# Block-sparse attention with an ELU feed-forward network: all 24 key blocks under a mask, or only the eight that a query block sees

## The chip, the cores and the metric

One core of a Trainium2 chip runs the whole program. The metric is device time in microseconds; lower is better. PE is TensorE, DVE VectorE, ACT ScalarE, POOL GpSimd, SP SyncE, which here only issues DMAs.

## What is computed

```python
B, H, S, D = 4, 8, 768, 64            # block = 32, so 24 blocks
scores = q @ k.T / sqrt(D)
mask = |blk_i - blk_j| <= 1           # neighbours
mask |= blk_i in (0, 23) or blk_j in (0, 23)
mask |= blk_j in sampled_blocks[blk_i]     # three drawn blocks per query block
attn = softmax(where(mask, scores, -1e9))
x = (attn @ v) as [3072 tokens, 512]
out = ELU(x @ w_in) @ w_out           # 512 -> 2048 -> 512
```
A query block from 1 to 22 sees at most eight key blocks: three neighbours, the first and the last, and three drawn ones, which may repeat others. Blocks 0 and 23 see all 24. The weights come as float64, the rest as float32; `sampled_blocks` is data, known only when the program runs.

## The kernel before

Every float32 operand of a product is held as two float16 parts, a high and a low one, and three of the four part products are summed. A batch has six tiles of 128 queries; two tiles are a chunk, so there are twelve chunks of 256 tokens. Work is queued by step with a rank within the step (`Steps`), and from step 40 on the order of emission is the order of issue on each engine. A chunk is 16 steps, one tile of one head each:

- `scores`: 128 queries against all 768 keys in four products, two key ranges by two parts of q. The two parts of k lie on the 128 rows with q twice.
- `sm_min` on DVE adds the mask and takes the row's minimum (scores come negated); `sm_exp` on ACT makes exp and its sum; `sm_hi` on ACT and `sm_lo` on DVE make the two parts of p, scaled by the reciprocal of the sum.
- `to_pT` transposes both parts of p with one DMA on SP's queue. `av_part` multiplies by v for a pair of heads: a first part with full array, a second with the two heads in the two column halves of the array (lines 365 and 371). `av_part3` is an earlier form for the first 32 tiles (line 348).
- `ffn_h`, `ffn_act1` to `ffn_act5` and `ffn_o` are the FFN of a chunk that is some ten steps behind: per chunk 192 products of 256 columns (line 426) and 96 of 512 (line 465).
- `load_w`, `w_bits1`, `w_bits2`, `w_split` turn a piece of the float64 weights into two float16 parts, 32 pieces, one per step in the first steps. `prep_k1/2`, `prep_v1/2`, `prep_q1/2` split the operands; k and q are transposed by DMA.
- `build_mask` and `expand_mask` make a mask of 128 queries by 768 keys for each tile of a batch, once.

Of the kernel before, what the change touches and what calls it, by code (L numbers as in the profile page):

```python
# [7 lines left out]
F32 = mybir.dt.float32  # L8
F16 = mybir.dt.float16
BF16 = mybir.dt.bfloat16  # L10
I32 = mybir.dt.int32
# [4 lines left out]
WINDOW = 1  # L16
# [3 lines left out]
class Steps:  # L20
    """Work queued by step; within a step the lower rank is issued first."""
# [16 lines left out]
    def left(self):  # L38
        return bool(self.work)


@with_exitstack
def kernel(
# [19 lines left out]
    NT = S // P            # query tiles (and key chunks) of a batch  # L63
    CT = 2                 # query tiles of a chunk
    NCH = NT // CT         # chunks of a batch
    NPAIR = H // 2
    DM, DFF = w_in.shape
# [3 lines left out]
    NB = S // BLOCK  # L71
    NR = sampled.shape[1]
    CW = CT * P            # tokens of a chunk
    HS = S * 2 // 3

    QS, KS, VS = -2.0, 16.0, 32.0
    SS = 2.0 ** 8          # scores come out as -SS * s
# [6 lines left out]
    assert abs(QS * KS) == SS / 8.0 and D == 64  # L84

    const = ctx.enter_context(tc.tile_pool(name="const", bufs=1))
    kvp = ctx.enter_context(tc.tile_pool(name="kvp", bufs=4))
    work = ctx.enter_context(tc.tile_pool(name="work", bufs=2))
    ps_s = ctx.enter_context(tc.tile_pool(name="ps_s", bufs=2, space=bass.MemoryType.PSUM))
    ps_a = ctx.enter_context(tc.tile_pool(name="ps_a", bufs=1, space=bass.MemoryType.PSUM))  # L90
    ps_f = ctx.enter_context(tc.tile_pool(name="ps_f", bufs=3, space=bass.MemoryType.PSUM))

    gs_col = const.tile([P, 1], F32, tag="gs", name="gs")
    nc.gpsimd.memset(gs_col, GS)
    st = Steps()
    chunks = [(b, c) for b in range(B) for c in range(NCH)]
    GSTEPS = 2 * CT        # steps of a (chunk, pair) group
    groups = [(t, hp) for t in range(len(chunks)) for hp in range(NPAIR)]
    NSTEP = len(groups) * GSTEPS

# [1 line left out]
    eqmb = work.tile([P, 2, S], BF16, tag="pT", bufs=4, name="eqmb")  # L102
    eq, mb = eqmb[:, 0, :], eqmb[:, 1, :]
    mask = const.tile([P, NT, S], BF16, tag="mask", name="mask")

    def build_mask():
        samp = const.tile([P, NR, 2], I32, tag="samp", name="samp")
# [3 lines left out]
        blk = const.tile([P, 3, NB], F32, tag="blk", name="blk")  # L111
        bi, bf, al = blk.bitcast(I32)[:, 0, :], blk[:, 1, :], blk[:, 2, :]
        nc.gpsimd.iota(bi, pattern=[[1, NB]], base=0, channel_multiplier=0)
        nc.gpsimd.memset(al, 1.0)
        for sg in (1, -1):
            nc.gpsimd.affine_select(
                al, al, pattern=[[sg, NB]], compare_op=ALU.is_ge, fill=0.0,
                base=WINDOW, channel_multiplier=-sg)
        for e in (0, NB - 1):
            nc.gpsimd.memset(al[:, e : e + 1], 1.0)  # L120
            nc.gpsimd.affine_select(
                al, al, pattern=[[0, NB]], compare_op=ALU.not_equal, fill=1.0,
                base=-e, channel_multiplier=1)
        # eq: 1 where the token (column) lies in the block (partition)
        nc.gpsimd.memset(eq, 1.0)
        eq3 = eq.rearrange("p (c k) -> p c k", c=NT)
        for sg, base in ((1, 0), (-1, BLOCK - 1)):
            nc.gpsimd.affine_select(
                eq3, eq3, pattern=[[sg, NT], [sg * NT, P]], compare_op=ALU.is_ge, fill=0.0,
                base=base, channel_multiplier=-sg * BLOCK)  # L130
        na = const.tile([P, P], BF16, tag="na", name="na")
        nc.gpsimd.memset(na, 0.0)
        nc.vector.tensor_copy(bf, bi)
        sf = const.tile([P, NR], F32, tag="sf", name="sf")
        nc.vector.tensor_copy(sf, samp[:, :, 0])
        for r in range(NR):
            nc.vector.scalar_tensor_tensor(
                al, bf, sf[:, r : r + 1], al, op0=ALU.is_equal, op1=ALU.add)
        nc.vector.tensor_scalar(na[:, :NB], al, 0.0, None, op0=ALU.is_le)
        # mb: rows key blocks, columns query tokens  # L140
        pm = ps_s.tile([P, 1024], F32, tag="s", name="pm")
        for n0, n1 in ((0, HS), (HS, S)):
            nc.tensor.matmul(pm[:, n0:n1], lhsT=na, rhs=eq[:, n0:n1], start=True, stop=True)
        nc.scalar.activation(mb, pm[:, :S], AF.Copy)

    def expand_mask(c):
        pm = ps_s.tile([P, 1024], F32, tag="s", name=f"pm{c}")
        for n0, n1 in ((0, HS), (HS, S)):
            nc.tensor.matmul(
                pm[:, n0:n1], lhsT=mb[:, c * P : (c + 1) * P], rhs=eq[:, n0:n1],  # L150
                start=True, stop=True)
        nc.scalar.activation(mask[:, c, :], pm[:, :S], AF.Copy, scale=NEG * SS)

# [1 line left out]
    wih, wil, woh, wol, wst = {}, {}, {}, {}, {}  # L155

    def load_w(i):
        f = i % NFC
        s = work.tile([P, 512, 2], I32, tag="wst", bufs=2, name=f"wst{i}")
# [9 lines left out]
    wu, wx = {}, {}  # L169

    def w_bits1(i):
        # 2^-111 on the upper word, read as float32, takes 888 off its exponent
        # field of 11 bits: what is left is the float32 field of 2^8 w.
        wu[i] = work.tile([P, 512], F32, tag="e", bufs=3, name=f"wu{i}")
        nc.scalar.activation(wu[i], wst[i].bitcast(F32)[:, :, 1], AF.Copy, scale=2.0 ** -111)
# [21 lines left out]
    kst, vst, qst = {}, {}, {}  # L197
    kT, vS, qT = {}, {}, {}

    def load_kv(b, hp, src, dst, nm):  # L200
        s = work.tile([P, 2 * NT, D], F32, tag="kvst", bufs=2, name=f"{nm}st{b}_{hp}")
        nc.sync.dma_start(
            s.rearrange("p (j c) d -> p j c d", j=2),
            src[b, 2 * hp : 2 * hp + 2].rearrange("j (p c) d -> p j c d", c=NT))
        dst[b, hp] = s

    nat = {}
# [7 lines left out]
    def prep_k1(b, hp):  # L215
        n = work.tile([P, 2 * NT, 2, D], F16, tag="knat", bufs=1, name=f"kn{b}_{hp}")
        nat["k", b, hp] = n
        hi_part(n[:, :, 0, :], kst[b, hp], KS)

    def prep_k2(b, hp):  # L220
        n = nat.pop(("k", b, hp))
        lo_part(n[:, :, 1, :], kst.pop((b, hp)), n[:, :, 0, :], KS)
        t = kvp.tile([P, 2 * NT, P], F16, tag="kT", name=f"kT{b}_{hp}")
        nc.sync.dma_start_transpose(t, n.rearrange("p a h d -> p (a h d)"))
        kT[b, hp] = t
# [3 lines left out]
    def v_part(t, j, hl):  # L229
        return t[:, j * NT : (j + 1) * NT, hl ^ j, :]  # L230

    def prep_v1(b, hp):
        t = kvp.tile([P, 2 * NT, 2, D], F16, tag="vS", name=f"vS{b}_{hp}")
        for j in range(2):
            hi_part(v_part(t, j, 0), vst[b, hp][:, j * NT : (j + 1) * NT, :], VS)
        vS[b, hp] = t

    def prep_v2(b, hp):
        t, s = vS[b, hp], vst.pop((b, hp))
        for j in range(2):  # L240
            lo_part(v_part(t, j, 1), s[:, j * NT : (j + 1) * NT, :], v_part(t, j, 0), VS)

    def load_q(t, hp):
        b, c = chunks[t]
        s = work.tile([P, 2 * CT, D], F32, tag="qst", name=f"qst{t}_{hp}")
        nc.sync.dma_start(
            s.rearrange("p (j c) d -> p j c d", j=2),
            q[b, 2 * hp : 2 * hp + 2].rearrange("j (p c) d -> p j c d", c=NT)[
# [367 lines left out]
```

## Time and profile before

| | |
|---|---|
| median of 3 runs | 874.04 us (873.43 to 877.04) |
| span of the profiled execution | 874.6 us |
| PE busy | 771.8 us (88%) |
| DVE busy | 728.7 us (83%) |
| ACT busy | 614.0 us (70%) |
| POOL busy | 213.1 us (24%) |
| DMA, SP's queue | 130.06 MB, 76.3% of 16 engines |
| mean granted clock of PE | 0.951 |

How to read it: the busy shares of the engines hold stages with different limits; the slices of the page and the windows show which engine is full when. PE's busy time comes from modelled ends of products that overlap, so the pace is read from the starts or from a run of many. An idle engine's wait is put down to what ended last.

### The profile page before, as it was taken

The page shows a single profiled execution, that of the slowest core. Times are in us where ns is not written, and L with a number is a line of the kernel's source. Part 1 is how long each engine was busy: PE and PEld are TensorE (multiplying, and loading weights), DVE is VectorE, ACT ScalarE, POOL GpSimd, SP SyncE. Part 2 cuts the span into 40 slices and gives each one's busy share as a digit, 9 for nine tenths or more (in the row PEclk, how much of TensorE's full clock was granted, in tenths as well). Part 3 has the DMA queues.
Part 4 walks back from the last instruction along what each step waited for, and adds up shares of the span by engine and source line. Part 5 has one row for each costly group of instructions (what it writes and reads, how often), then busy time and mean ns, then how long its engine had stood idle before and what let it go on. Part 6 is the DMA issues. An engine that isn't in the chain of part 4 may idle for free.

```text
span 874.6 us, 15351 instructions
## 1 busy us (share of the span) xinstructions
PE 771.8 (88%) x5486; PEld 505.9 (58%) x5486; DVE 728.7 (83%) x1526; ACT 614.0 (70%) x1088; POOL 213.1 (24%) x170
## 2 busy tenths in 40 slices
PE   2455457889987999999979999999989999999998
PEld 0123245447745756757746757758548658567583
DVE  5999999998997887987997988969989969879130
ACT  5866567778877867867767867767878769677140
POOL 3565656620210210210210211301201202103030
PEclk9765688999999999999999999999999999999999
DMA  8998989779999587799997778699897786776000
GB/s 223 244 213 196 200 186 218 182 161 157 183 215 207 101 146 151 119 165 181 178 191 158 139 145 140 121 186 170 164 226 145 134 160 124 144 140 108 23 13 25
DMA packets 412912, 137.33 MB, mean 157 GB/s; under 512 B 379044, under 2 KB 407716, under 8 KB 412836
## 3 DMA queue, kind: packets, MB, share of 16 engines
q1 hardware_dynamic: 409380, 130.06, 76.3%
q10 hardware_dynamic: 3456, 6.29, 2.3%
q8 instruction: 43, 0.70, 0.3%
q14 instruction: 33, 0.27, 0.1%
HBM read 35.65 MB, written 6.29 MB: 48 GB/s over the span
## 4 chain that ended last, share of the span: by engine, by line
PE 50%; DVE 14%; DMA 4%; ACT 2%; issue 1%; ACTq 0%; DVEq 0%
PE o L465 19%; PE h L426 18%; PE s L281 7%; DVE p L319 5%; PE av L365 4%; DMA pT<-p 4%; DVE t L290 3%; PE av L371 2%; DVE e L444 1%; DVE gh L449 1%; DVE kn L213 1%; DVE xf L405 1%; DVE vS L213 1%; ACT t L297 1%; ACT p L307 0%
## 5 line engine op out<-in xcount | busy, mean ns | idle before, releaser
L454 POOL TENSOR_TENSOR gl<-e,gh 128x512 f16<-128x512 f32 x96 | 121.2, 1263 | 572.6 <-DVE gh L449 446.6
L307 ACT ACTIVATE p<-t,sum 128x768 f16<-128x768 f32 x168 | 157.0, 934 | 122.9 <-DVE sum L303 90.2
L290 DVE CUSTOM_DVE_ANT_0 t<-s,mask 128x768 f32<-128x768 f32 x192 | 182.5, 951 | 52.7 <-PE s L281 51.5
L281 PE MATMUL s<-kT,qT 128*128 128x512 f16 (+1 forms) x768 | 167.2, 343 | 58.3 <-DVE m L290 39.2
L426 PE MATMUL h<-xl,wih 128*128 128x256 f16 x768 | 210.7, 275 | 2.6 <-DVE xl L389 2.6
L426 PE MATMUL h<-xh,wih 128*128 128x256 f16 x768 | 209.6, 274 | 3.6 <-DVE e L444 2.0
L426 PE MATMUL h<-xh,wil 128*128 128x256 f16 x768 | 210.8, 275 | 0.0
L319 DVE SCALAR_TENSOR_TENSOR p<-t,sum,p 128x768 f16<-128x768 f32 x168 | 208.2, 1239 | 1.5 <-ACT p L307 1.5
L297 ACT ACTIVATE t<-t,m 128x768 f32<-128x768 f32 x192 | 177.2, 923 | 7.9 <-DVE m L290 7.7
L426 PEld LDWEIGHTS <-wih 128*128 128x128 f16 x1536 | 149.5, 98 | 27.8 <-issue 9.7
L281 PEld LDWEIGHTS <-qT 128*128 128x128 f16 x768 | 76.5, 101 | 125.5 <-issue 41.5
L465 PE MATMUL o<-wol,gh 128*128 128x512 f16 x384 | 145.8, 380 | 1.0 <-POOL wol L194 1.0
L465 PE MATMUL o<-woh,gh 128*128 128x512 f16 x384 | 146.0, 380 | 0.1
L465 PE MATMUL o<-woh,gl 128*128 128x512 f16 x384 | 145.8, 380 | 0.0
L465 PEld LDWEIGHTS <-gh 128*128 128x128 f16 x768 | 73.6, 98 | 77.0 <-issue 4.5
L444 DVE SCALAR_TENSOR_TENSOR e<-h,e 128x512 f32<-128x512 f32 x96 | 66.0, 688 | 34.3 <-ACT e L440 33.6
L426 PEld LDWEIGHTS <-wil 128*128 128x128 f16 x768 | 75.7, 99 | 12.3 <-issue 3.0
L365 PE MATMUL av<-pT,vS 128*128 128x256 f16 x480 | 62.9, 279 | 13.2 <-DMA pT<-p 13.1
L440 ACT ACTIVATE e<-e,gs 128x512 f32<-128x512 f32 x96 | 69.3, 722 | 2.9
L434 ACT ACTIVATE e<-h 128x512 f32<-128x512 f32 x96 | 55.9, 582 | 19.0 <-PE h L426 14.5
L465 PEld LDWEIGHTS <-gl 128*128 128x128 f16 x384 | 37.6, 98 | 45.9 <-issue 1.3
L365 PEld LDWEIGHTS <-vS 128*128 128x128 f16 x480 | 47.3, 100 | 22.4 <-DMA pT<-p 14.1
(59 smaller groups left out, 782.2 us busy)
## 6 DMA issues: line engine op xcount, KB each, us to landing
wst<-in_moe_w_in_dram SPq DMA_DIRECT2D x16, 512.0 KB, 4.5
wst<-in_moe_w_out_dram SPq DMA_DIRECT2D x16, 512.0 KB, 4.1
qst<-in_q_dram SPq DMA_DIRECT2D x48, 128.0 KB, 3.0
kst<-in_k_dram SPq DMA_DIRECT2D x16, 384.0 KB, 3.8
vst<-in_v_dram SPq DMA_DIRECT2D x16, 384.0 KB, 3.9
out_dram<-r ACTq DMA_DIRECT2D x24, 256.0 KB, 3.2
pT<-p SPq DMA_TRANSPOSE x192, 4.0
qT<-qn SPq DMA_TRANSPOSE x48, 3.4
```

Source lines behind the costliest of these rows:

```text
L281: nc.tensor.matmul(ps[:, n0:n1], lhsT=qT[t, hp][:, (j * CT + c) * 2 + hl, :], rhs=kk[:, n0:n1], start=(hl == 0), stop=(hl == 1))
L290: nc.vector.tensor_tensor_reduce(ts_, pS.pop(i)[:, :S], mask[:, chunks[t][1] * CT + c, :], op0=ALU.add, op1=ALU.min, scale=1.0 / SS, scala ...
L297: nc.scalar.activation(tS[i], tS[i], AF.Exp, bias=mS.pop(i), scale=-1.0, accum_out=s)
L307: nc.scalar.activation(p[:, 0, :], tS[i], AF.Copy, scale=sumS[i])
L319: nc.vector.scalar_tensor_tensor(p[:, 1, :], tS.pop(i), sumS.pop(i), p[:, 0, :], op0=ALU.mult, op1=ALU.subtract)
L365: nc.tensor.matmul(o[:, j, :], lhsT=vv[:, j * NT + kc, :, :].rearrange("p h d -> p (h d)"), rhs=pT[t, hp, j][:, kc, :], start=(kc == 0 and ...
L426: nc.tensor.matmul(ps[:, e, :], lhsT=w[2 * f + e][:, cs], rhs=x[t][:, cc, :], start=(n == 0), stop=(n == 3 * NCC - 1))
L434: nc.scalar.activation(e, hS[t, f], AF.Exp, scale=IH)
L440: nc.scalar.activation(e, e, AF.Relu, bias=gs_col, scale=-GS)
L444: nc.vector.scalar_tensor_tensor(e, hS.pop((t, f)), -IH * GS, e, op0=ALU.mult, op1=ALU.min)
L454: nc.gpsimd.tensor_tensor(g, eS.pop((t, f)), gh[f], op=ALU.subtract)
L465: nc.tensor.matmul(o, lhsT=g[f][:, e, ms], rhs=w[2 * f + e], start=(f == 0 and e == 0 and n == 0), stop=(f == NFP - 1 and e == 1 and n == 2))
```

## The change

Attention is written anew; the FFN, the weights' conversion and the splitting into two parts stay as they are in their arithmetic.

- Tokens 32 to 735 of a batch (blocks 1 to 22) are cut into six units of four query blocks, the last with two; the first and last block go apart (`special`), as 64 queries against all keys. A unit (`unit`) handles four heads: two pairs, each with one head on rows 0 to 63 and one on rows 64 to 127.
- `gather_k` copies, for each query block and drawn block, 32 keys of the transposed k next to each other on DVE. The place comes from a register, loaded from the list of drawn blocks (`block_of`). `gather_v` does the same for v with a DMA from a scratch tensor in device memory into `vg`; v is split first and stored there (`store_v`).
- `scores` has one product for each query block, head and part, on 64 rows by 32 columns of the array, against 96 neighbour keys, 64 edge keys or 96 drawn keys. `attn_v` has one for each query block, head and half of the 256 keys, on 128 rows by 32 columns.
- A row of p has 256 keys instead of 768. Its division by the sum moves behind the product with v (`norm`). The mask shrinks to eight values per query.
- The order of issue is fixed from the start. A chunk is still 256 tokens and 16 steps; its FFN begins 21 steps after its attention.

```diff
+    def block_of(eng, qb, r):
+        c = qb * NR + r
+        return eng.value_load(idx[0:1, c : c + 1], min_val=0, max_val=NB - 1)
...
+    def gather_v(b, u, i):
+        qb = 1 + QB * u + i
+        t = vg[slot[b, u]]
+        nc.sync.dma_start(t[0:96, 0, i], scr[b][(qb - 1) * BLOCK : (qb + 2) * BLOCK, :])
+        for r in range(NR):
+            n = block_of(nc.sync, qb, r)
+            nc.sync.dma_start(
+                t[32 + 32 * r : 64 + 32 * r, 1, i], scr[b][bass.ds(n * BLOCK, BLOCK), :])
+
+    def gather_k(b, u, qd):
+        n = blocks_in(u)
+        t = work.tile([P, 4, QB * NR * BLOCK], F16, tag="kR", name=f"kR{b}_{u}_{qd}")
+        kR[b, u, qd] = t
+        for c in range(n * NR):
+            x = block_of(nc.vector, 1 + QB * u + c // NR, c % NR)
+            nc.vector.tensor_copy(
+                t[:, :, c * BLOCK : (c + 1) * BLOCK],
+                kT[b, qd][:, :, bass.ds(x * BLOCK, BLOCK)])
...
+    def scores(b, u, qd):
...
+        for pp in range(2):
+            for part in range(3):
+                for ql, kl in PROD:
+                    kb = kk[:, 2 * pp + kl, :]
+                    for i in range(n):
+                        w0 = (QB * u + i) * BLOCK
+                        for j in range(2):
+                            js = slice(64 * j, 64 * j + 64)
...
+                            nc.tensor.matmul(
+                                ps[32 * i : 32 * i + 32, j, pp, c0:c1],
+                                lhsT=qT[b, u][
+                                    js, 2 * (2 * qd + pp) + ql, q0 + 32 * i : q0 + 32 * i + 32],
+                                rhs=m, start=(ql + kl == 0), stop=(ql == 1))
...
+    def attn_v(b, u, qd):
...
+                for e in range(6):
+                    ab, (pl, vl) = e // 3, PROD[e % 3]
+                    for i in range(n):
+                        nc.tensor.matmul(
+                            o[32 * i : 32 * i + 32, h, :],
+                            lhsT=t[:, pl * 8 + (2 * j + pp) * 2 + ab, 32 * i : 32 * i + 32],
+                            rhs=vv[:, ab, i, h, vl, :], start=(e == 0), stop=(e == 5))
...
+    LEAD = 21
+    NSTEP = 2 * NFP
+    E0 = 8
...
+        st.at(s - 1, 3.0, lambda: gather_k(b, u, qd))
+        st.at(s, 0, lambda: scores(b, u, qd))
+        st.at(s, 5, lambda: sm_min(b, u, qd))
+        st.at(s, 6, lambda: sm_exp(b, u, qd))
+        st.at(s + 1, 3.1, lambda: sm_hi(b, u, qd))
+        st.at(s + 1, 3.2, lambda: sm_lo(b, u, qd))
+        st.at(s + 1, 8, lambda: sm_T(b, u, qd))
+        st.at(s + 4, 1, lambda: attn_v(b, u, qd))
```

On DVE, one tile in the steady part before: minimum and its value, the reciprocal of the sum, the low part of p.

```order
L290 ISA t_4521,m_4522<-s_4468,mask 128x768
L290 ISA m_4522 128x1
L302 TENSOR_SCALAR sum_4512<-sum_4512 128x1
L303 RECIPROCAL sum_4512<-sum_4512 128x1
L319 SCALAR_TENSOR_TENSOR p_4510<-t_4440,sum_4462,p_4510 128x768
```
On DVE now, around the gather for a half unit in the second batch (`kR` is the gathered k; the load, the two checks, the address step and the copy stand six times for a half unit, twelve for a full one):

```order
L364 ISA t_4_1_9839,m_4_1_9840<-s_4_1_9661,mask 128x256
L364 ISA m_4_1_9840 128x1
L564 SCALAR_TENSOR_TENSOR e_3_9905<-h_3_9806,e_3_9905 128x512
L569 CAST gh_3_9909<-e_3_9905 128x512
L120 TENSOR_LOAD idx
L120 ISA x2
L318 ISA
L318 COPY kR_5_0_9913<-kT_0_5853 128x4x32
L394 SCALAR_TENSOR_TENSOR p_4_1_9974<-t_4_1_9839,p_4_1_9974 128x1024
```
The minima shrink from 768 to 256 columns, and the register loads and copies come between the FFN's work and the low part of p.

On SP's queue before, in the steady part, transpositions of p, k and q with an operand's load between:

```order
L314 DMA_TRANSPOSE pT_4601<-p_4603 128x12x128
L224 DMA_TRANSPOSE kT_0_4669<-kn_0_4607 128x12x128
L202 DMA kst_1_4677<-in_k_dram 128x2x384
L314 DMA_TRANSPOSE pT_4736<-p_4671 128x12x128
L263 DMA_TRANSPOSE qT_0_4740<-qn_0_4675 128x8x128
```
And now, where the gathers of v for a unit (`vg`) stand among the transpositions:

```order
L402 DMA_TRANSPOSE pT_5_0_10292<-p_5_0_10289 128x16x64
L306 DMA vg_80<-scr_4704 96x1024
L120 TENSOR_LOAD idx
L120 ISA x2
L309 ISA
L309 DMA vg_80<-scr_4704 32x1024
L280 DMA_TRANSPOSE qT_2_10571<-qn_2_10500 128x8x128
```
The load, the checks, the address step and the gather stand three times for each query block; the transpositions queue behind them.

On PE before, one tile's scores between the FFN's products (rows that only repeat are left out; there are four pairs of load and product):

```order
L465 LDWEIGHTS gl_1_4766
L465 MATMUL o_1_5205<-woh_997,gl_1_4766 128x512
L281 LDWEIGHTS qT_1_4992
L281 MATMUL s_5226<-kT_1_4921,qT_1_4992 128x512
L281 MATMUL s_5226<-kT_1_4921,qT_1_4992 128x256
L465 LDWEIGHTS gh_2_4820
```
And now a full unit's scores, followed by the product with v of an earlier unit (144 and 96 pairs):

```order
L546 MATMUL h_6_12286<-xT_9625,wil_1277 128x256
L351 LDWEIGHTS qT_3_11681
L351 MATMUL s_3_1_12447<-kT_1_5855,qT_3_11681 32x96
L351 MATMUL s_3_1_12447<-kT_1_5855,qT_3_11681 32x64
L351 MATMUL s_3_1_12447<-kR_3_1_12319,qT_3_11681 32x96
L417 LDWEIGHTS pT_3_0_12236
L417 MATMUL av_3_12592<-vg_81,pT_3_0_12236 32x64
```
Where four wide pairs stood at each step, a block of 288 short rows and one of 192 stand at one step of four. PE has 29582 rows in all, before 10974.

More of the change, by code (lines that the diff above doesn't have):

```diff
@@ L15 @@
 BLOCK = 32
-WINDOW = 1
 NEG = 1e9
@@ L91 @@
     ps_f = ctx.enter_context(tc.tile_pool(name="ps_f", bufs=3, space=bass.MemoryType.PSUM))
+    ctx.enter_context(tc.manual_schedule())
+    st = Steps()
     gs_col = const.tile([P, 1], F32, tag="gs", name="gs")
     nc.gpsimd.memset(gs_col, GS)
[L95 to L102, printed above, removed]
@@ L139, in build_mask @@
[L139 to L152, printed above, removed]
+        nc.vector.tensor_copy(idx, idx2.rearrange("p (a t) -> p a t", t=2)[:, :, 0])
@@ L269, in where @@
-    def where(i):
-        t, hp = groups[i // GSTEPS]
-        j, c = divmod(i % GSTEPS, CT)
-        return t, hp, j, c
-    def scores(i):
-        t, hp, j, c = where(i)
-        b = chunks[t][0]
-        ps = ps_s.tile([P, 1024], F32, tag="s", name=f"s{i}")
-        kk = kT[b, hp][:, j * NT : (j + 1) * NT, :].rearrange("p c k -> p (c k)")
-        for n0, n1 in ((0, HS), (HS, S)):
-            for hl in range(2):
-                nc.tensor.matmul(
-                    ps[:, n0:n1], lhsT=qT[t, hp][:, (j * CT + c) * 2 + hl, :], rhs=kk[:, n0:n1],
-                    start=(hl == 0), stop=(hl == 1))
-        pS[i] = ps
@@ L583 @@
+    prep_lo("q", 0, 0)
+    prep_qT(0, 0)
+    for c in range(NK):
+        prep_hi("k", 0, c)
+        prep_lo("k", 0, c)
+        for qd in range(NQ):
+            prep_kT(0, c, qd)
+    build_mask()
+    for c in range(NK):
+        st.at(c, 3.6, lambda c=c: prep_v_hi(0, c))
+        st.at(c, 3.7, lambda c=c: prep_v_lo(0, c))
+        st.at(c, 8.5, lambda c=c: store_v(0, c))
+    for s in range(max(st.work) + 1):
         if s in st.work:
             st.run(s)
-        s += 1
+    assert not st.work
```

683 lines of the change are left out of this document (384 added, 299 removed).

## The prediction

> **What bounds the kernel now.** I read the page first (busy shares, the slices, the chain that ended last), then one stage by windows, then the chain in order of time, then single groups.
>
> ```profile
> span 874.6 us, 15351 instructions
> PE 771.8 (88%) x5486; PEld 505.9 (58%) x5486; DVE 728.7 (83%) x1526; ACT 614.0 (70%) x1088; POOL 213.1 (24%) x170
> PE   2455457889987999999979999999989999999998
> PEclk9765688999999999999999999999999999999999
> PE 50%; DVE 14%; DMA 4%; ACT 2%; issue 1%; ACTq 0%; DVEq 0%
> ```
> The profiled span is 0.6 us over the median of the runs, 874.04. PE is full from about slice 9 on and half idle before; the clock is cut only there too. So two stages: a start of some 150 us that PE does not set, and a long steady stage.
>
> ```profile
> 0.00:60.00 60.00, 25.32 (x108) 11.63 (x108) 50.45 (x98) 39.94 (x69) 28.09 (x33) 0.80 0.96 226
> 60.00:120.00 60.00, 30.35 (x176) 17.03 (x177) 59.22 (x102) 37.80 (x66) 35.91 (x23) 0.63 0.91 203
> 120.00:180.00 60.00, 44.91 (x351) 30.40 (x351) 60.00 (x107) 43.27 (x76) 38.95 (x24) 0.94 0.87 192
> 653.00:714.00 61.00, 61.00 (x450) 41.23 (x449) 52.98 (x121) 46.01 (x83) 9.91 (x8) 1.00 0.78 149
> ```
> Columns after the length: PE, PEld, DVE, ACT, POOL busy, the clock, DMA share, GB/s. In the start DVE is busy 94% of 180 us: it bounds there. In the steady stage PE is busy 61.00 of 61.00 us and DVE 52.98.
>
> ```profile
> 652.88 2.69 PE o L465 x12
> 713.73 2.70 PE o L465 x12
> 774.58 2.70 PE o L465 x12
> 829.43 20.96 PE h L426 x192
> 850.39 20.73 PE o L465 x96
> ```
> The same piece of the FFN comes back every 60.85 us: that is one chunk of 256 tokens. Twelve chunks are 730 us; 144 us of the span are start and end. Undisturbed, a chunk's FFN takes 20.96 + 20.73 = 41.7 us (0.109 us for a product of 256 columns, 0.216 for 512), and attention the other 19.2 of PE. The FFN does not change, so 41.7 us per chunk is the floor: what can be won is 19 us of 61.
>
> **PE after the change.** Per batch there are ten full units (128 queries, half of the heads) and two half ones, so 3.67 full units to a chunk. A unit's scores are 144 products on an eighth of the array each (64 rows by 32 columns), 18 waves of eight; its product with v is 96 products on a quarter, 24 waves of four. The nearest row is the second part of the old product with v, two halves of the array side by side:
>
> ```profile
> 510.15:510.95 0.80, 0.78 (x12) 0.58 (x12) 1.00 0.52 96
> L371 PE MATMUL av<-pT,vS 128*64 128x256 f16 x480 | 33.8, 277 | 0.0
> L371 PEld LDWEIGHTS <-vS 128*64 128x64 f16 x480 | 23.1, 109 | 8.6 <-issue 8.6
> ```
> Twelve products lasted 0.78 us, the last alone 0.277: six pairs start within 0.50 us, 0.10 us per pair of 256 columns, what one whole product takes. So parts of the array do run side by side. By columns a wave of 96 takes 0.041 us and one of 64 takes 0.027: 12 x 0.041 + 30 x 0.027 = 1.3 us per unit. From above: if each wave lasts as long as one weight load (0.109), 42 x 0.109 = 4.6. I take 0.05 a wave, nearer the columns, because the pair hid its loads: 2.1 us, and four changes of the array's form at 0.1 each (below, 0.20 us between neighbours of different forms where 0.11 is usual), 2.5 per unit, 9.2 per chunk. First and last block: 4 us a batch (24 wide products twice, four at a time, and 72 of 64 columns twice, two at a time), 1.3 per chunk. PE: 41.7 + 9.2 + 1.3 = 52.2 us.
>
> The unknown is whether so many short instructions arrive fast enough: PE's rows rise from 10974 to 29582.
>
> ```profile
> 15.57 0.14 PEld L143 LDWEIGHTS <-na 128*128 128x128 bf16 x2 [15.57 <-POOL wil L194]
> 15.60 0.80 PE L143 MATMUL pm<-eqmb,na 128*128 128x512 bf16 x2 [15.60 <-DVE na L139]
> L143 PEld LDWEIGHTS <-na 128*128 128x128 bf16 x2 | 0.1, 103 | 15.6 <-POOL wil L194 15.6
> 97.97 0.27 PE L348 MATMUL av<-pT,vS 128*64 128x256 f16 x1
> 98.17 0.28 PE L426 MATMUL h<-xh,wil 128*128 128x256 f16 x1
> ```
> Here PE starts from empty. The second load ends at 15.71 and lasts 0.103, so it starts 0.037 us after the first, with a product between: at most 18 ns an instruction. That is an upper bound: 480 instructions a unit x 18 = 8.6 us, and PE would need 41.7 + 31.7 + 1.3 = 75 us per chunk. The lower bound is the 1.3 us above. I take the lower side, because nothing in the row shows a delay, and carry the upper as a rival. [...]
>
> **DVE after the change.** Per chunk, with the part that does not depend on size set at 0.15 us (the rows with one column):
>
> ```profile
> L319 DVE SCALAR_TENSOR_TENSOR p<-t,sum,p 128x768 f16<-128x768 f32 x168 | 208.2, 1239 | 1.5 <-ACT p L307 1.5
> L290 DVE CUSTOM_DVE_ANT_0 t<-s,mask 128x768 f32<-128x768 f32 x192 | 182.5, 951 | 52.7 <-PE s L281 51.5 <-POOL p L334 0.6
> L290 DVE DVE_READ_ACCUMULATOR2_ANT m<- 128x1 f32 x192 | 15.6, 81 | 0.0
> L444 DVE SCALAR_TENSOR_TENSOR e<-h,e 128x512 f32<-128x512 f32 x96 | 66.0, 688 | 34.3 <-ACT e L440 33.6
> L449 DVE CAST gh<-e 128x512 f16<-128x512 f32 x96 | 40.9, 426 | 0.3
> L213 DVE SCALAR_TENSOR_TENSOR kn<-kst,kn 128x768 f16<-128x768 f32 x16 | 17.1, 1070 | 3.0 <-ACT kn L210 3.0
> L303 DVE RECIPROCAL sum<-sum 128x1 f32<-128x1 f32 x192 | 31.1, 162 | 5.3
> L302 DVE TENSOR_SCALAR sum<-sum 128x1 f32<-128x1 f32 x192 | 28.4, 148 | 10.2 <-ACT t L297 8.7
> L261 DVE COPY qn<-qn 128x512 f16<-128x512 f16 x48 | 18.1, 377 | 1.4
> L181 DVE SCALAR_TENSOR_TENSOR wx<-wst,wx 128x512 int32<-128x512 int32 x32 | 33.7, 1053 | 0.1
> L180 DVE TENSOR_SCALAR wx<-wu 128x512 int32<-128x512 int32 x32 | 28.6, 894 | 0.4 <-ACT wu L175 0.3
> L183 DVE SCALAR_TENSOR_TENSOR wx<-wu,wx 128x512 int32<-128x512 int32 x32 | 27.5, 860 | 0.1
> ```
> Minima: 16 of 256 columns at 0.42 + 0.08, 8.0 us. Low parts of p: 4 of 1024 at 1.6, 6.4. FFN: 8 x (0.688 + 0.426), 8.9. Operands: 6 of 512 at 0.76, 4.6. Norm: 2 x (0.15 + 0.16 + 0.69), 2.0. First and last block: 1.33 x (0.95 + 0.15 + 0.31 + 1.24), 3.5. Sum 33.4, against 53 now. Added: 44 copies of 128 columns, 0.2 each between 0.15 and L261's 0.377, 8.8: DVE busy 42.2.
>
> Ahead of each copy stand a load of a register, two checks and an address step; before has none. Lower bound: 0.08 us, the shortest instruction of DVE (L290's second). Upper: 3.0, a round trip to memory by DMA:
>
> ```profile
> qst<-in_q_dram SPq DMA_DIRECT2D x48, 128.0 KB, 3.0
> 0.80 0.45 SPq L246 DMA_DIRECT2D qst<-in_q_dram  x1
> 655.36 1.23 SPq L263 DMA_TRANSPOSE qT<-qn  x1
> ```
> Nearest is the 0.45 us in which a queue's sequencer works out one DMA; a load also waits for an answer: I take twice that, 0.9. [...] While a load runs, DVE's sequencer can only hide it behind work already handed to the engine. Not hidden at all, a gather is 0.9 with the copy before it underneath: 33.4 + 44 x 0.9 = 73 us per chunk. All hidden: 42.2. No row tells which, so I take the middle, 57.6. That is over PE's 52.2: DVE becomes the bound, and PE waits for kR at the head of scores, with the FFN's products queued behind it.
>
> **SP.** It issues 160 transpositions in all where it issued 256, and gains 264 gathers of v with a register load each. Per chunk 22 x (0.45 + 0.9) + 16.7 plain DMAs x 0.5 + 13.3 transpositions x 1.23 = 54.5 us of issue, in order, and a transposition of p queues behind up to a dozen gathers. Close to DVE's figure, still under it. ACT and POOL lose work and bound nothing; bytes moved fall with the transpositions.
>
> **Start and end.** FFN begins 29 steps in (8 + 21), a chunk is 16 steps, attention ends at about step 201, so 172 steps (10.75 chunks) have both and 20 have FFN alone. In the first 29 DVE has the weights, 33.7 + 28.6 + 27.5 = 89.8, 13 operand pieces 9.9, the small mask 25 x 0.15 = 3.8, the first loads about 5 (a landing of 3.0, ACT's part and the issue), and 5.25 units at 11.1 (2.0 + 1.6 + 0.9 and 12 gathers at 0.55): 167 us. The weights' work on DVE lies on the path of the start now and after. Sum: 167 + 10.75 x 58 + 20/16 x 41.7 + 3.5 (last matmul to end, as now) = **846 us**.
>
> **The rivals.**
> *Loads hidden, PE bounds.* The sequencer stays ahead of a DVE that waits for PE. Then 10.75 x 52.2 and a start shorter by 5.25 x 12 x 0.35 = 22: 765 us. For it: DVE now waits 51.5 us for scores (L290). Against: twelve loads stand in a row. [...]
> *Loads not hidden* (the other side): 73 a chunk, start 189: 189 + 785 + 56 = 1030. It decides against the change from 61 us a chunk, that is, where under about 40% of the 0.9 is hidden.
> *PE's stream too slow* (the other side): place, the scores' 288 rows in a block. From 8.3 ns an instruction it passes DVE, from 10 it passes 60.85 us; at 13, 931 us, at 18, 1029. Parts of the array that ran one after another would cost about as much: 240 products by columns are 8 us a unit.
> *Given back by order.* From scores to the product with v there are four steps, 14.5 us; minimum, exp, the parts of p and the transposition fill some 10 to 13, and SP may come 3 late. If each unit stalls PE by a microsecond or two, a chunk is back at 61 us and the time at about 874.
>
> **How the numbers follow.** A measurement of this kernel tells about 0.5% (870 to 878) from no change. The forecast (DVE or SP at 53 to 62 us a chunk, 790 to 885) has 0.49, of which 0.38 is faster, 0.06 the same by order, 0.05 slower. Hidden loads 0.15, faster. PE's stream 0.19 and open loads 0.17, slower. So faster 0.53, same 0.06, slower 0.41. The range runs from 760 (a little under the PE bound) to 1000, which leaves out the far end of the two slow rivals; the forecast's own range is 790 to 885.
>
> **What will show it.** A chunk's period near 58 us between the same FFN pieces; DVE busy about 42 a chunk with idle time before kR; the register loads' length; products of one wave starting a few ns apart and a unit's scores about a microsecond long. Wrong if loads last over 1.3 us, if a unit's scores pass 3 us with no wait, or if PE waits longest for transposed p (then SP or order is the cause).

## The result and the profile after

The changed kernel takes 1331.16 us (median of four runs, 1326.84 to 1332.53), the kernel before 873.73 on the same chip (872.65 to 877.04): 1.522 times as long (95% interval 1.518 to 1.526). The forecast was 846, its range 760 to 1000.

The page of the changed kernel, with the rows that stood in the prediction for the kernel before (the slices and the clock in tenths, the chain by engine) and one more, of the DMA queue that the page names instruction (packets, MB, share):

```profile
span 1330.5 us, 37235 instructions
PE 766.6 (58%) x14790; PEld 514.5 (39%) x14790; DVE 538.1 (40%) x1497; ACT 408.8 (31%) x862; POOL 198.4 (15%) x162
PE   0011123676546767676546667676446667676798
PEclk9999976777777877777777778778777787778799
PE 10%; DVEq 4%; DVE 4%; issue 3%; ACT 2%; SPq 1%; DMA 1%; ACTq 0%; POOL 0%; POOLq 0%
q8 instruction: 115, 1.88, 0.7%
```
No engine is full anywhere. DVE did lose its work (538 us busy against 729), but PE is busy only 58% of the span, at a cut clock from slice 6 on. A kernel in which nothing is full is bound by waits, so the next view is the waits (us in all, times, longest):

```profile
PE s L351 <- DVE kR L318: 365.4, 155, 21.6
PE s L351 <- DMA qT<-qn: 40.0, 11, 16.1
PE s L351 <- DMA kT<-kn: 39.8, 3, 13.6
PE av L417 <- DMA pT<-p: 0.4, 1, 0.4
...
DVE kR L318 <- issue: 298.2, 480, 1.4
```
PE stands 365 us in front of scores for the gathered k (84 of them in the first 201 us, 281.6 later), and DVE 298 us in front of its copies with no other engine to blame: in 480 places, 0.6 us each. Both engines can be seen in one unit, DVE first (rows in between are left out):

```profile
1065.94 0.43 DVE L569 CAST gh<-e 128x512 f16<-128x512 f32 x1
1066.71 1.10 DVE L318 COPY kR<-kT 128x128 f16 x2 [0.35 <-issue]
1069.86 0.20 DVE L318 COPY kR<-kT 128x128 f16 x1 [0.59 <-issue]
1075.73 0.20 DVE L318 COPY kR<-kT 128x128 f16 x1 [0.58 <-issue]
1075.86 0.69 DVE L564 SCALAR_TENSOR_TENSOR e<-h,e 128x512 f32<-128x512 f32 x1
```
```profile
1066.02 0.27 PE L546 MATMUL h<-xT,wil 128*128 128x256 f16 x1
1066.22 0.56 PE L351 MATMUL s<-kT,qT 64*32 64x96 f16 x48
1075.97 0.42 PE L351 MATMUL s<-kR,qT 64*32 64x96 f16 x18 [2.45 <-DVE kR L318]
1076.12 0.68 PE L351 MATMUL s<-kT,qT 64*32 64x96 f16 x48
1076.99 1.47 PE L417 MATMUL av<-vg,pT 128*32 128x64 f16 x96
1078.40 0.61 PE L546 MATMUL h<-xT,wih 128*128 128x256 f16 x2
1078.80 0.42 PE L546 MATMUL h<-xT,wil 128*128 128x256 f16 x1
1081.13 0.27 PE L546 MATMUL h<-xT,wil 128*128 128x256 f16 x1
1081.24 0.38 PE L546 MATMUL h<-xT,wih 128*128 128x256 f16 x2
```
Twelve copies of 0.20 us (the first took 1.00), one each 0.787 us: a register load (0.303 in the median of the trace), register arithmetic for the address (0.19 and 0.06) and gaps go ahead of each. They start when the FFN's last conversion of the step is done and take 9.5 us; PE issues its last FFN product at 1066.02, does what needs no gathered k, takes the rest piece by piece as copies come, and has the last of them at 1075.97. When it goes on it is slow: the FFN products of 256 columns start 0.20 us apart at 1078.4 and 0.11 apart again at 1081.1, and the granted clock, 1.00 from 1060.0 to 1070.0, falls to 0.61 from there to 1073.0, while PE waits, and is 0.50 from there to 1078.4, 0.52 to 1081.0 and 1.00 in the next two microseconds. From the restart to the normal pace it is about 5 us.

Cut at each chunk's first FFN product, windows (length; busy of PE, PEld, DVE, ACT, POOL; clock, DMA share, GB/s): three of the changed kernel's eleven with the sum and mean of all, then two of the kernel before:

```profile
201.15:323.93 122.78, 72.08 (x1468) 47.92 (x1465) 52.30 (x158) 40.15 (x91) 17.04 (x14) 0.74 0.41 87
433.43:518.89 85.46, 59.79 (x986) 39.78 (x984) 35.70 (x92) 29.08 (x54) 13.59 (x10) 0.82 0.42 90
921.83:1031.12 109.29, 60.85 (x1249) 41.13 (x1248) 38.91 (x115) 29.68 (x65) 13.89 (x10) 0.75 0.55 118
sum 1083.41, PE 701.39 PEld 469.31 DVE 425.26 ACT 334.96 POOL 149.97; mean PE 63.76 PEld 42.66 DVE 38.66 ACT 30.45 POOL 13.63
```
```profile
54.43:204.27 149.84, 99.94 (x673) 60.18 (x673) 146.75 (x275) 103.41 (x180) 80.43 (x52) 0.82 0.89 193
339.21:400.06 60.85, 60.85 (x451) 41.14 (x448) 52.08 (x116) 45.81 (x83) 9.91 (x8) 1.00 0.83 144
```
The FFN begins at 201.15 us; eleven chunks take 1083.41 (98.5 each); the last takes 45.9 to the end. The kernel before begins at 54.43, but its first chunk lasts 149.84 under the weights; its next ten take 62.5 each. So 120 us were lost up to the second chunk (323.9 against 204.3), 336 in the ten chunks after it (96.1 against 62.5), 0.6 at the end.

### The profile page after: what moved, and what is told of

Same layout as the page of the kernel before. It is cut to its first block, busy times and chain, and to the rows that moved or that the text cites. A ratio compares the mean times of both kernels' runs of the same rounds, so it can differ in the third digit from the quotient of the medians.

```text
span 1330.5 us, 37235 instructions
## 1 busy us (share of the span) xinstructions
PE 766.6 (58%) x14790; PEld 514.5 (39%) x14790; DVE 538.1 (40%) x1497; ACT 408.8 (31%) x862; POOL 198.4 (15%) x162
## 3 DMA queue, kind: packets, MB, share of 16 engines
q8 instruction: 115, 1.88, 0.7%
## 5 line engine op out<-in xcount | busy, mean ns | idle before, releaser
L546 PE MATMUL h<-xT,wih 128*128 128x256 f16 x1536 | 298.5, 301 | 0.0
L351 PE MATMUL s<-kR,qT 64*32 64x96 f16 x2112 | 72.5, 259 | 365.6 <-DVE kR L318 365.4
L318 DVE COPY kR<-kT 128x128 f16 x528 | 126.5, 243 | 335.5 <-issue 298.2
L351 PEld LDWEIGHTS <-qT 64*32 64x32 f16 x6336 | 74.6, 102 | 484.5 <-issue 440.4
L546 PE MATMUL h<-xT,wil 128*128 128x256 f16 x768 | 229.4, 299 | 0.6 <-issue 0.6
L380 ACT ACTIVATE t<-t,m 128x256 f32<-128x256 f32 (+1 forms) x192 | 95.3, 498 | 419.4 <-DVE m L364 419.4
L394 DVE SCALAR_TENSOR_TENSOR p<-t,p 128x1024 f16<-128x1024 f32 (+1 forms) x48 | 60.8, 1266 | 91.0 <-ACT p L388 91.0
L417 PE MATMUL av<-vg,pT 128*32 128x64 f16 x4224 | 69.4, 236 | 21.6 <-issue 21.2
L417 PEld LDWEIGHTS <-pT 128*32 128x32 f16 x4224 | 60.2, 125 | 31.3 <-issue 26.0
L364 DVE CUSTOM_DVE_ANT_1 t<-s,mask 128x256 f32<-128x256 f32 (+1 forms) x192 | 69.6, 418 | 5.2 <-PE s L351 4.7
```

The lines of the kernel that those rows point to most:

```text
L318: nc.vector.tensor_copy(t[:, :, c * BLOCK : (c + 1) * BLOCK], kT[b, qd][:, :, bass.ds(x * BLOCK, BLOCK)])
L351: nc.tensor.matmul(ps[32 * i : 32 * i + 32, j, pp, c0:c1], lhsT=qT[b, u][js, 2 * (2 * qd + pp) + ql, q0 + 32 * i : q0 + 32 * i + 32], rhs= ...
L364: nc.vector.tensor_tensor_reduce(t[:n, j, pp, :].rearrange("p (a b) -> p a b", b=BLOCK), ps[:n, j, pp, :].rearrange("p (a b) -> p a b", b= ...
L380: nc.scalar.activation(t[:n, j, pp, :], t[:n, j, pp, :], AF.Exp, bias=m[:n, j, pp : pp + 1], scale=-1.0, accum_out=s[:n, h : h + 1])
L394: nc.vector.scalar_tensor_tensor(p[:n, 1, :], tS.pop((b, u, qd))[:n].rearrange("p j g k -> p (j g k)"), PS, p[:n, 0, :], op0=ALU.mult, op1 ...
L417: nc.tensor.matmul(o[32 * i : 32 * i + 32, h, :], lhsT=t[:, pl * 8 + (2 * j + pp) * 2 + ab, 32 * i : 32 * i + 32], rhs=vv[:, ab, i, h, vl, ...
```

## The experiments

Two theories to begin with. **G**: the gather of k, with a register load ahead of each copy, stands in DVE's order in front of scores, and PE waits in its own order. **O**: the order of the new attention (four steps from scores to the product with v, SP's queue) holds PE, and would without a gather. Times are medians with the 95% interval of the ratio to the kernel before, which took 873.6 to 876.1 beside them. Eleven of the eighteen runs leave a part of the attention out, as said at each; they show what that part costs.

### Is it the gather?

**Copies from fixed places**, so no register loads on DVE (the wrong keys are read):
```diff
-            x = block_of(nc.vector, 1 + QB * u + c // NR, c % NR)
+            x = (3 + 5 * c) % NB
```


> The gather of k copies from fixed places: 528 copies stay, their register loads go; the drawn keys are wrong ones. Theory G (the gather of a unit lies bare between the FFN's work of one step and the scores of the next, 12 x 0.787 us): a unit's gather falls to 12 x 0.2 = 2.4 us or less, 44 units gain 7 us each, about 310 us, and PE's clock recovers a part: 960 to 1030 us. Rival O (the order on SP's queue, late transpositions of p, makes the steps long): over 1200 us.

Measured 1092.6 us (1.238 to 1.259): 239 less, where G had named 960 to 1030. PE still waits 92.7 us for the copies.

**No gather at all**; the scores read 96 keys of k itself (wrong ones):
```diff
-        st.at(s - 1, 3.0, lambda: gather_k(b, u, qd))
...
-        kk, kr = kT[b, qd], kR.pop((b, u, qd))
+        kk = kr = kT[b, qd]
```


> No gather of k at all: the drawn part of the scores reads fixed keys in k itself. Theory G: the whole 9.4 us per unit goes, about 415 us, and the waits for kR with it: 860 to 950 us; what then stays over 767 us is something else (start, first and last block, SP). Rival O: over 1150 us.

Measured 1066.63 (1.203 to 1.234): 265 of the 457 us are the gather, and 239 of these the register loads and address work, 26 the copies. But G had expected 950 or less, and some 190 us stay. PE's waits, the start's long ones (34.9, 23.7) among them:

```profile
PE av L417 <- DMA pT<-p: 80.6, 10, 34.9
PE s L351 <- DMA qT<-qn: 76.5, 10, 23.7
PE s L351 <- DMA kT<-kn: 39.4, 3, 13.4
PE av L417 <- issue: 38.2, 18, 4.2
```
The wait for transposed p, 0.4 us with the gather, is 80.6 without it, 34.8 of them behind the first 200 us. The gather had covered a second limit, so both theories hold a part.

**The same loads and copies, three at each of the four steps before**, on DVE, and then on POOL (the whole attention in both):
```diff
+        parts = 1 if (u, qd) == (0, 0) else 4
+        for g in range(parts):
+            st.at(s - parts + g, 3.0, lambda g=g: gather_k(b, u, qd, g, parts))
```


> The same loads and copies on DVE, but three at each of the four steps ahead of the scores instead of twelve at the last. Theory G as place (the wait is exposed because it stands in a block): DVE then needs 33 + 44 x 0.79 = 68 us per chunk and bounds, about 950 to 1050 us. If the loads' own time on DVE's stream is what counts and the place is not, over 1200 us, because each step's FFN work waits behind three loads and PE behind it.

> As the spread gather, but on POOL, which is 85% idle. Theory G: DVE is rid of it, POOL has 12 + 44 x 0.8 = 47 us per chunk, PE 52: 830 to 930 us. Rival O: over 1150 us. If POOL's copies and loads are much slower than DVE's (over 1.2 us an item), POOL bounds at 65 us per chunk or more and the time is over 950 us.

Measured 1213.27 (1.375 to 1.398) and 1125.8 (1.277 to 1.296). With the same instructions on the same engine, 118 us are due to the block of twelve alone. But the time lies in the range named for the case that the place does not count (over 1200), and PE still waits 247.4 us for kR: a little more than half of the gather's 265 us stays. Spread on POOL, 205 are gone, where G had named 830 to 930. An item takes 0.71 us there in the median, so slow items on POOL are not the reason; PE still waits 189.8 us for POOL's kR. It is the whole attention at its best so far, and far from 874.

**One register load for both quads of a unit**, still in a block, copying to both tiles:
```diff
+            for qd in range(NQ):
+                nc.vector.tensor_copy(
+                    kR[b, u, qd][:, :, c * BLOCK : (c + 1) * BLOCK],
+                    kT[b, qd][:, :, bass.ds(x * BLOCK, BLOCK)])
```


> Only the sharing: one register load for both halves of the heads, all in a block at the step ahead of a pair's first scores. 264 loads of 0.59 us with their address work fewer on DVE: if the bare gather sets the time, a pair's 18.9 us become 12 x 1.0 to 1.1 = 12 to 13 us, 22 pairs gain 6 each, 130 us: 1180 to 1220. If the loads are hidden or only the copies count: 1310 to 1340.

Measured 1216.88 (1.389 to 1.397), within the 1180 to 1220 expected. Half of the 528 loads less is worth 114 us, 0.43 us for each of 264, against about 0.59 of idle time ahead of a copy.

### The register loads on SP

Both without the gather of k. First **v gathered from fixed places**, so no register loads on SP (wrong rows of v); then **v's gather, with its loads, on POOL's queue**:
```diff
-            n = block_of(nc.sync, qb, r)
+            n = (qb + 5 + 6 * r) % NB
```


> No gather of k, and the gathers of v go to fixed places: the 264 register loads on SP's queue go, their DMAs stay. An item falls from about 1.1 us of SP to about 0.4. Theory S (what is left over PE's 52 us a chunk without the gather of k is SP's queue, late at the turns of the batches): PE's waits for transposed q, k and p shrink, the cadence of the chunks falls from 76 to 60 to 68 us, 900 to 980 us. Rival L (the steps are long because of latency from scores to the product with v, whatever SP does): no change, 1050 to 1075.

> No gather of k; the gathers of v with their register loads move from SP's queue to POOL's, which is 80% idle. Theory S: SP is rid of 33 us per chunk, 880 to 980 us. Rival L: 1050 or more; if POOL's own issue is much slower than SP's, the product with v waits for vg and the time rises.

Measured 1014.24 (1.150 to 1.173) and 1053.3 (1.202 to 1.209). SP's loads cost 52 us, less than theory S had named (900 to 980). With loads and gathers on POOL's queue 39 of the 52 stay; the 13 that are gone lie within the intervals. Another run combined shared loads on DVE, spread, with v on POOL's queue, for the whole attention:

> All of attention computed. One register load serves both halves of the heads (264 loads on DVE, 528 copies), three per step over four steps, and the gathers of v are on POOL's queue. By the sum of what the two halves showed: gather of k 22 x 0.9 = 20 us of DVE per chunk instead of 35, SP free: cadence 65 to 80 us, 950 to 1090 us. If DVE's stream is the bound of everything, as with the spread gather: 1100 to 1200.

Measured 1164.59 (1.328 to 1.338), 39 more than the gather spread on POOL, and in the range named for DVE's stream as the bound.

### What holds the other 140 us?

From here on the base is the run of 1014 us, which gathers no k and reads v at fixed places. Three explanations were tried. **Q**: SP is late, since it stands 119 us for x ahead of the transpositions behind it. x one step later:
```diff
-            st.at(s + 5, 8, lambda: x_T(b, u, t, c0))
+            st.at(s + 6, 8, lambda: x_T(b, u, t, c0))
```


> This is the kernel without the gather of k and with v's rows at fixed places (1014 us), and now the transposition of x stands one step later in SP's order. In the 1014 us kernel SP stands 118.6 us in front of that transposition, waiting for the low part of x from POOL, with the transpositions of p, k and q queued behind it; PE waits 190 us in all for transposed p, q and k (some 85 of it in the start). Theory Q (what is left is SP's order): SP's wait falls under 40 us, PE's waits for transposed tiles fall by 40 or more, 950 to 985. Rival F (what is left is the start and the fetching of PE's instructions, its gaps named issue at multiples of 256 instructions, 62 us): 1000 to 1020, within 1.5%.

Measured 1025.82 (1.167 to 1.175), 12 more, within the two intervals, where Q had named 950 to 985. SP's waits in the base, and in this run:

```profile
SPq L457 <- POOL xn L451: 118.6, 20, 12.6
SPq L402 <- DVE p L394: 69.0, 23, 13.2
```
```profile
SPq L457 <- POOL xn L451: 6.0, 1, 6.0
SPq L402 <- DVE p L394: 176.3, 23, 13.1
```
The wait went from x to p, the next in SP's order: SP was waiting for the units, not the units for SP. Q falls in this form. Two runs on top of it, with k's preparation three steps earlier (`s = e0 + 6 + c` for `e0 + 9 + c`, four buffers for kT), and with v gathered for the first chunk only:

> As the run with x one step later, and the next batch's k loaded, split and transposed three steps earlier, with a fourth buffer for the transposed k. In the 1014 us kernel the chunks at a change of batch last 82, 85 and 90 us, the others 56 to 68. Theory Q: the three long chunks fall by 10 to 20 each, a further 30 to 50 us. Rival F: within 10 us of the run with x one step later.

> As the run with x one step later, but v's rows are gathered for the first chunk alone and used for all (left out: 220 of 240 gathered blocks of v, the tokens get wrong rows): SP loses 80 to 90 us of issue a batch and the transfers of v. Theory Q: SP is no longer late, 30 to 60 us under the run with x one step later. Rival F: if the fetching of PE's instructions competes with these transfers, PE's gaps named issue fall from some 60 us to under 30 and the time by as much, while PE's waits for transposed tiles stay; if it does not compete, within 10 us.

Measured 1007.45 (1.145 to 1.156) and 995.23 (1.126 to 1.139): 18 and 31 less than with x later, the first under the 30 to 50 that Q had named, the second at the low end of its 30 to 60. PE's wait named issue ahead of the products with v is 42.0 us in the second and 39.4 without it, so v's transfers are not what makes it. What v's gathers cost, issue on SP or traffic, this does not tell. The whole attention with shared loads on POOL and x later was no gain either:

> The whole attention: k is gathered by POOL, one register load serves both quads, spread over up to four steps, and x is transposed one step later. Gather theory: POOL's spread gather took 1126; half of the register loads less is some 500 x 0.5 us on POOL, of which PE now waits 190 us in front of scores for; together with x later 1040 to 1090. If the loads' length did not matter any more (only the order does): 1090 to 1126.

Measured 1139.54 (1.289 to 1.309), 14 more than spread without sharing, within the intervals, where 36 to 86 less had been expected.

**A**: ACT stands, in order, in front of loads of the next batch's v and k, with the units' exponentials behind it. Six staging buffers for two, loads four steps ahead for two:
```diff
-                st.at(s - 2, 9, lambda b=b + 1, c=c: load_v(b, c))
+                st.at(s - 4, 9, lambda b=b + 1, c=c: load_v(b, c))
```


> The kernel without the gather of k and with v's rows at fixed places (1014 us), and now the loads of the next batch's k and v are issued four steps ahead instead of two, into six staging buffers instead of two. Theory A (ACT stands in front of late loads, 58.1 + 28.9 us, and holds the exponentials, p, SP's queue and PE behind it): these waits fall under 20 us, the three long chunks fall from 82 to 90 us to 68 to 75, the time to 950 to 975. Rival F (the chunks at a change of batch are long because of the transpositions of k and the fetching of PE's instructions): 1000 to 1014.

Measured 990.41 (1.130 to 1.139), 24 less. ACT's waits in the base, and in this run:

```profile
ACT vN L251 <- DMA stv<-in_v_dram: 58.1, 9, 10.6
ACT kn L251 <- DMA stk<-in_k_dram: 28.9, 6, 6.5
```
```profile
ACT vN L251 <- DMA stv<-in_v_dram: 6.6, 4, 2.2
ACT kn L251 <- DMA stk<-in_k_dram: 2.4, 1, 2.4
```
The wait is gone, 78 us of it, and the time fell by 24: the three chunks at a change of batch went from 82, 85 and 90 us to 78, 81 and 83, not to 68 to 75. The mechanism is there; the price was a third. The same with v gathered once, and the same (three steps, three buffers) in the whole attention with the gather on POOL:

> As the run with loads ahead, and v's rows are gathered for the first chunk alone and used for all (left out: the other gathers of v). Theory A with SP free of the gathers: 925 to 955; what is left over 874 is then the start, first product of the FFN at some 183 us against 54 (about 55 us net of the slow first chunk of the kernel before). Rival F: 980 to 995, as with v gathered once and the loads two steps ahead (995).

> The whole attention: k is gathered by POOL, three blocks at each of the four steps before the scores (1126 us so), and the loads of the next batch's k and v are issued three steps ahead into three buffers. Theory A: one more step of about 4 us on each of 15 waits that sum to 93 us: 40 to 60 us less, 1065 to 1085. Rival F: 1115 to 1126.

Measured 971.39 (1.107 to 1.117) and 1108.99 (1.263 to 1.272), 19 and 17 less; both lie between the ranges of A and of its rival. The second is the fastest whole attention of the new kind that was run.

**F**: PE waits for its own instructions. In the run of 971 us:

```profile
363.25 1.37 PE L351 MATMUL s<-kT,qT 64*32 64x96 f16 x144
364.55 0.99 PE L417 MATMUL av<-vg,pT 128*32 128x64 f16 x94
368.70 0.21 PE L417 MATMUL av<-vg,pT 128*32 128x64 f16 x2 [3.17 <-issue]
479.01 0.61 PE L417 MATMUL av<-vg,pT 128*32 128x64 f16 x30
481.84 1.09 PE L417 MATMUL av<-vg,pT 128*32 128x64 f16 x66 [2.22 <-issue]
```
PE stops in the middle of a unit, whose operands are all there, once after 94 products and once after 30. Numbered over all of PE's weight loads and products, 25 of the 43 places behind 200 us where two neighbours start more than 0.8 us apart stand at 183 to 185 over a multiple of 256, 58.7 of 119.8 us. 115 packets with 1.88 MB (the row of q8 above) are 16.3 KB each; if each carries 256 instructions, they are 115 x 256 = 29440, close to PE's 29582 rows. That is an estimate: no trace shows what a packet holds. By F bursts of half the length stop less, so the next run issues each unit's products in two halves with 24 FFN products between them:
```diff
+        st.at(s, 0, lambda: scores(b, u, qd, (0,)))
+        st.at(s, 2.05, lambda: scores(b, u, qd, (1,)))
...
+        st.at(s + 4, 1, lambda: attn_v(b, u, qd, (0,)))
+        st.at(s + 4, 2.06, lambda: attn_v(b, u, qd, (1,)))
```


> As the run with loads ahead and v gathered once (971 us; left out: the gathers of k and the later gathers of v); each unit's scores and product with v are issued in two halves, the second half behind the 24 FFN products (2.6 us) of the step. Theory F (PE's instruction fetch cannot follow 480 instructions in 3 us): the gaps at one remainder of 256 fall from some 58 us to under 30, the time by 15 to 30: 940 to 956. Rival L (the gaps are something else, and the 2.6 us more from scores to the product with v count): gaps as before, 971 to 990.

Measured 1038.2 (1.181 to 1.189), 67 more. PE's waits in the run of 971 us, and in this one:

```profile
PE av L417 <- DMA pT<-p: 49.4, 13, 34.7
PE av L417 <- issue: 45.8, 20, 3.7
```
```profile
PE av L418 <- DMA pT<-p: 108.3, 27, 37.1
PE av L418 <- issue: 7.8, 3, 4.0
```
F's gaps did go, 46 to 8 us, and no remainder of 256 has more than five of the 45 gaps that are left. That a stop is a fetch of instructions is not itself in the trace; its place and its going with the burst speak for it. But scores end 2.6 us later, all that follows them too, and PE waits 59 us more for transposed p. Behind the first 200 us it is 57.4 us in 25 waits against 4.9 in 11, so these waits are some 2.3 us each: in four steps the chain from scores to the product with v has no slack to take 2.6 us more. PE's own busy time also rose by 25 us (709.4 against 684.3), and its waits for transposed q, and for the first and last block's p, by 13 and 10. So both are true, and the second is the dearer. It shows what a longer chain costs; in the run of 971 us, with 4.9 us of such waits behind the start, the chain is just met.

Last, the FFN three steps nearer to its attention (`LEAD = 18`), and both edits in the whole attention with loads ahead:

> As the run with loads ahead and v gathered once, and the FFN follows its attention three steps earlier (18 steps instead of 21). Theory S (the start is a row of steps of some 6 us ahead of the FFN): the first FFN product falls from 181 to about 163, the time by 10 to 20: 951 to 961. Rival L (x comes too late for it, PE waits for it in every chunk): a chunk gains as much as the start loses, 971 or more.

> The whole attention with k gathered by POOL in portions and the loads three steps ahead (1109 us), now with each unit's products in two halves and the FFN three steps earlier. If theories F and S both hold: 25 to 45 less, 1064 to 1084. If neither, 1100 to 1130. In no case near 874, since PE still waits for POOL's gather.

Measured 999.83 (1.137 to 1.149) and 1284.7 (1.455 to 1.471), 28 and 176 more. The FFN's first product came at 172.6 us instead of 181.4, and PE then waited 45.2 us for x, for which it does not wait in the run of 971 us: the 21 steps are needed. The last run was forecast at 1064 to 1130: each of its two edits lengthens or tightens the chain, and PE waits longer for POOL's gather as well (245.4 us for 174.1 in the run of 1109 us). Which of the two cost more in it was not taken apart.

## Why the prediction was wrong

The lost 457 us by the runs: 239 DVE's register loads and address work, 26 its copies, 52 the loads on SP, 24 the late loads of k and v, 19 v's other gathers, and 97 that stay (971 against 874). They were taken away in this order; in another, the shares would be others. Of the 97, the start holds some 53 by the trace (the second chunk begins at 257.2 us in that run, at 204.3 before); no run took it away. Behind the first 200 us PE's waits there are 50 us named issue, 43 for transposed k and q, and 5 for p.

- **PE after the change: right.** 2.5 us were forecast for a unit; 144 products of scores take 1.37 us from end to end and 96 with v about 1.0 to 1.5 in the rows above. A product of scores with its weight load every 9.5 ns is 4.8 ns an instruction: the bound of 18 ns was far. A chunk of the run of 971 us that had full clock shows PE busy for 55.5 us, against 52.2 forecast:

```profile
609.17:666.30 57.13, 55.48 (x1465) 39.19 (x1464) 30.27 (x82) 32.88 (x80) 14.88 (x10) 1.00 0.63 123
```
- **DVE's busy time and the item's length: right in size.** Forecast 42.2 a chunk, measured 38.7; an item 0.9 us, measured 0.787; a copy 0.2, measured 0.20. The item came out partly by luck: 0.9 was twice the issue of a DMA, given to the load alone. The load takes 0.303, and register arithmetic of 0.25 and gaps, which the sum did not name, make up the rest.
- **"Half hidden": wrong.** Only the copy itself lies under the next load, as in the prediction's side without hiding: in the trace a load starts some 23 ns after the start of the copy before it, and 0.59 us of idle time stand ahead of nearly every copy. A copy of 0.20 us is done long before the next one, 0.787 us behind it. Of the twelve copies of the unit above only the first, which lasted 1.00 us, covers all of the next load and its arithmetic (1066.74 to 1067.47). That half of the load time could be hidden was the prediction's estimate, and the trace does not show it. (By its own terms the rival "loads hidden" adds up to 762 us, not 765.)
- **The chunk as the larger of PE and DVE: wrong, and the largest error.** 58 us a chunk were forecast, 98.5 measured, though both engines were sized well. Even with no load hidden DVE's stream is 38.7 + 44 x 0.59 = 64.7 us a chunk, so the larger of the two sums could not have given it. Measured, behind the first 201 us, are 63.8 us of PE's work and 25.6 of its wait for kR; the other 9.1 are other waits. The gather of a unit stands, in DVE's order, between the FFN's conversions of one step and the next, and PE's FFN products stand, in PE's order, behind scores. So PE has at most one piece of 2.6 us to do against 9.5 us of gather, each full unit (in the unit above that piece was over when the gather began), and 365 us of wait came on top of PE's own work. The prediction did name the wait, PE at the head of scores for kR, but not its price. The rival "loads not hidden" had the bare loads at 0.17, but it too let DVE's 73 us run beside PE and stopped at 1030. And none of the three signs of being wrong came: they ask for sizes and for p, and the error lay in how the sums go together.
- **The clock: not in the sum.** For the same 14790 products PE is busy 766.6 us here and 680.6 in the base without register loads, where the clock is 0.929 against 0.815. Of the 86 us, 37 are the FFN's products, which are the same in both (580.1 us against 543.5): PE goes slower because it waits, as in the unit above, where the clock fell from 1.00 to 0.50 in a wait and stayed at 0.50 to 0.52 for some 5 us after it. The rest is attention's, where products that stand alone behind a copy add to the busy time too.
- **SP and order: under-priced.** SP's register loads cost 52 us, though in the run with them SP itself still waits 65.6 us for x and 64.9 for p. "Given back by order" was put at about 874; without any register load or gather of k 1014 are left, and the runs after it, on order, loads and v, took away 43 of the 140.
- **The start: 167 forecast, 201 measured.** The units of the start wait for gathers that stand in DVE's order among the weights, up to 21.6 us at a time:

```profile
56.94 0.26 PE L351 MATMUL s<-kR,qT 64*32 64x96 f16 x2 [21.55 <-DVE kR L318]
83.29 0.26 PE L351 MATMUL s<-kR,qT 64*32 64x96 f16 x2 [17.77 <-DVE kR L318]
144.37 0.26 PE L351 MATMUL s<-kR,qT 64*32 64x96 f16 x2 [19.09 <-DVE kR L318]
```
Without the gather it is 182.7, so half of the error was the gather again.

Still open: the rest of the start, and what the order would cost with neither PE's gaps nor the longer chain; a fifth step from scores to the product with v, with the buffers that it needs, was not tried.

## What to carry to other kernels

Two engines that waited for each other in order added their times within a step here (63.8 us of PE's work and 25.6 of its wait for kR in a chunk of 98.5), though their busy shares were 58% and 40%: size a step by the work of the one that stands in the other's path, and take the larger of two sums only where each has other work queued ahead. A gather by register offsets costs the load and the address work per block and per engine (0.6 us here for a copy of 0.2), so share the load, spread the items over steps, or put them on an engine that is less in the way: 114, 118 and (spread, on POOL) 205 us here, each by itself; combined they did not add up. Before moving work within a fixed number of steps, count what slack the chain through them has: 2.6 us more in one link cost 67 us here.

## What the chip showed that was not expected

- PE can stop with its operands there: with bursts of 480 instructions in 2.5 us, 25 stops of 1.2 to 3.9 us stood within two of the same remainder of 256 instructions, 58.7 us in one run; with FFN products between the halves of the bursts they were gone. That PE ran out of instructions is the author's explanation; no trace shows it itself.
- A register load from a tile in on-chip memory lasts 0.303 us on VectorE and 0.270 on SyncE in the median; with its register arithmetic and gaps it sets a pace of 0.787 us with a copy and some 1.11 us with a DMA issue.
- Products on 64 rows by 32 columns of the array, eight places side by side: a unit's 144, each with its weight load, take 1.37 us, 9.5 ns each. One after another, at the FFN's pace of 256 columns in 0.109 us, they would be some 5.2 us (an estimate).
